# First pair of an attention and gated-MLP kernel on zero-padded operands, extra TensorE products, and a planner with backward passes

## The chip, the cores and the metric

The kernel runs on one core of a Trainium2 chip. The metric is device time in microseconds (us) of one execution. The core's engines run side by side, each with its own queue of instructions, and wait for one another by semaphores: TensorE (PE in the profile; PEld is its weight load), VectorE (DVE), ScalarE (ACT), GpSimd (POOL), and SyncE (SP), whose queue here issues all transfers.

## The reference

Self-attention with queries averaged in pairs, and behind it an MLP with a spatial gate. Batch 8, 8 heads, 1152 keys, 576 pooled queries, head size 64, all f32.

```python
q_pool = q.reshape(B, H, S // 2, 2, D).mean(axis=3)
scores = np.matmul(q_pool, k.transpose(0, 1, 3, 2)) / np.sqrt(D)
attn = np.exp(scores - np.max(scores, axis=-1, keepdims=True))
attn = attn / (np.sum(attn, axis=-1, keepdims=True) + 1e-09)
x = heads_merged(np.matmul(attn, v))          # (8, 576, 512)
h = np.maximum(x @ w_in, 0.0)                 # (8, 576, 1024)
u, g = h[..., :512], h[..., 512:]
g = (g - mean(g)) / np.sqrt(var(g) + 1e-06)   # over the last axis
g = np.einsum('ts,bsd->btd', w_spatial, g) + b_spatial[None, :, None]
out = (u * g) @ w_out                         # (8, 576, 512)
```

## The kernel before

**Pairs.** Attention goes over 32 pairs of heads (i = 0 to 31, four pairs to a batch). f32 operands are split in two f16 numbers, a head and a residual, so that products run at f16 rate. For each pair:

- `prep(i)` loads queries and keys of both heads, stacked on 128 partitions (64 for each head), sums the query pairs on POOL, takes sums of squares on ACT, derives power-of-two scales (`scales`: one tiny product, three DVE steps), and makes heads (`head`, ACT) and residuals (`rest`, DVE, or POOL). Products want head and residual of one attention head stacked on the 128 rows, so transfers copy rows between partitions: `khi` (key heads twice), `qhi` (query head over query residual), `klo` and `xq` (key residual against query head in 64 rows, and two rows more that carry the shift of the softmax).
- `maxima(i)` forms the scores' heads in 27 products of 128 queries by 384 keys (9 query tiles by 3), each reduced by DVE (L751) out of a PSUM bank. Banks `pm` (two) and, in the first unit, `pw` (two) take turns. For pairs 0 and 1 (`DIRECT = 2`) the first head's products (t < 4) read `xq` and the plain key heads `kn` on 64 rows; t = 4 mixes both heads through `qd`; the rest read the copied `qhi` and `khi`.
- `shift` turns the maxima into the two f16 rows of the shift: four DVE steps, a transposing product (L773), a copy (L775), two transfers into `xq` (L778). It runs behind t = 4 and behind the last tile.
- `attention(i)` makes 18 key tiles of exact scores by two products each (L950 on 128 rows, L951 on 66), an exp on ACT (L956) and a subtraction on POOL (L976) that leaves the low half of each f32 in its place. The 64 queries left over of each head are four tail tiles (L963, L967, L972). `values` multiplies high and low halves by head and residual of v, four products each (L853, L859, L864; L846 in f32 for three key tiles of nine in pairs 0 to 7).

**Scheduling of generators.** While `attention(i)` steps, `maxima(i + 1)`, the values' preparation, `prep(i + 2)` and the input weights' conversion (`in_weights`, from pair 0 on at 0.14 steps a tick) step beside it. After two batches a `gated_unit` does the MLP for them, at half a step a tick, in `pw`.

**What sets the order.** The program order of these generators is only the input of a planner, `Order.pin`. It gives each instruction a cost, goes through time, and at each step takes for the engine that is free first the earliest instruction in program order whose inputs are due. "Due" adds an allowance (`SLACK`) to the modelled end where the result crosses to TensorE: 1400 ns from POOL, 300 from ACT, 400 from DVE, 1000 from SP. The order found is fixed for each engine; the hardware's queues then run in it, each waiting at its head. ACT's order up to the end of `prep(0)` and SP's order up to `order.line` are held as written.

**The start.** As written: loads of pair 0, four loads of v, `prep(0)` whole (the next pair's loads among its last steps), 18 steps of `maxima(0)`, the sums of squares of v, the rest of `maxima(0)`, `prep(1)`, the weights' first loads, the first split of v.

## Time and profile before

| | us |
|---|---|
| median of 3 runs | 1167.14 |
| the runs | 1171.51, 1166.41, 1167.14 |
| profiled execution, its time | 1172.69 |
| profiled execution, its span | 1170.9 |
| TensorE busy | 1139.1 (97%) |
| ACT, DVE, POOL busy | 891.6, 858.7, 846.5 |

The page's busy time of TensorE runs from a matmul's start to its end, and matmuls overlap, so rates are read from the distance of two starts. Slices of 1/40 of the span show TensorE at 40% and 90% or more of the first two, and at 90% or more from then on but for the last; the granted clock (PEclk, tenths of full speed) is 7 in the second slice, 9 in the first and full behind it.

### The profile page before, as it was taken

To read this page: it belongs to the slowest core of one execution; us is meant where nothing else is said; L and a number is where in the kernel's file an instruction comes from. 1 tells how busy PE (TensorE), PEld (TensorE's weight loads), DVE (VectorE), ACT (ScalarE), POOL (GpSimd) and SP (SyncE) were. 2 spreads that over 40 slices of the span, in tenths; PEclk is the share of its full clock that TensorE was granted. 3 is DMA by queue.
4 is the path that set the end of the run, shared out by engine and by line. 5 is a ranking of instruction groups with operands and counts; after the bars stand their busy time and mean duration, and the time that the engine had idled before them with its cause. 6 is when DMAs were issued, how large, how long until landed. Compare 5 with 4: busy or idle time off the path is not lost.

```text
span 1170.9 us, 33542 instructions
## 1 busy us (share of the span) xinstructions
PE 1139.1 (97%) x13297; PEld 723.9 (62%) x13297; DVE 858.7 (73%) x2240; ACT 891.6 (76%) x1697; POOL 846.5 (72%) x732
## 2 busy tenths in 40 slices
PE   4999999999999999999999999999999999999998
PEld 1567777776566666666666666666666666665453
DVE  5699999867899878766678668866668777832644
ACT  6698789988787978788777977978777877754423
POOL 3566566778887988889787978898788877883000
PEclk9799999999999999999999999999999999999999
DMA  6575456444432443565323454265433431121002
GB/s 217 153 210 147 111 164 205 139 118 139 125 107 73 122 144 103 140 180 143 90 71 85 139 133 122 69 168 163 115 104 82 127 88 20 38 65 37 1 1 81
DMA packets 88990, 132.97 MB, mean 114 GB/s; under 512 B 39872, under 2 KB 48064, under 8 KB 88832
## 3 DMA queue, kind: packets, MB, share of 16 engines
q1 hardware_dynamic: 88832, 130.82, 39.8%
q8 instruction: 104, 1.70, 0.6%
q14 instruction: 54, 0.44, 0.1%
HBM read 81.20 MB, written 9.44 MB: 77 GB/s over the span
## 4 chain that ended last, share of the span: by engine, by line
PE 82%; DVE 7%; DMA 4%; ACT 3%; POOL 1%; issue 1%; SPq 1%; DVEq 0%; ACTq 0%; POOLq 0%
PE pss L950 9%; PE pss L951 9%; PE pm L745 8%; PE pw L1190 7%; PE pw L1147 7%; PE pw L1103 6%; PE pw L1036 6%; PE o L853 5%; PE o L864 5%; PE o L859 5%; DVE mt L751 3%; PE o L846 2%; PE pss L1036 1%; PE pss L1147 1%; DMA kt<-in_kT_dram 1%; PE pss L1190 1%
## 5 line engine op out<-in xcount | busy, mean ns | idle before, releaser
L976 POOL TENSOR_TENSOR pt<-pt 128x512 f16<-128x512 f32 x528 | 580.9, 1115 | 173.2 <-ACT pt L956 167.8
L956 ACT ACTIVATE pt<-pss,esc 128x512 f32<-128x512 f32 x576 | 389.2, 690 | 115.4 <-PE pss L951 107.9
L751 DVE TENSOR_REDUCE mt<-pm 128x1 f32<-128x384 f32 x733 | 387.5, 549 | 106.3 <-PE pm L745 90.6
L950 PE MATMUL pss<-qhi,khi 128*128 128x512 f16 x576 | 220.6, 383 | 3.9 <-ACT ptl L972 2.1
L951 PE MATMUL pss<-xq,klo 66*128 66x512 f16 x576 | 221.1, 384 | 0.0
L745 PE MATMUL pm<-khi,qhi 128*128 128x384 f16 x643 | 198.1, 326 | 5.2 <-DMA khi<-kn 3.4
L853 PEld LDWEIGHTS <-pt 128*128 128x128 bf16 x2112 | 125.1, 99 | 68.4 <-issue 3.0
L853 PE MATMUL o<-vp,pt 128*128 128x65 f16 x2112 | 157.3, 193 | 1.5 <-DVE xm L872 1.5
L864 PE MATMUL o<-vp,pt 128*128 128x65 f16 x2112 | 154.7, 193 | 0.0
L859 PE MATMUL o<-vp,pt 128*128 128x64 f16 x2112 | 153.1, 193 | 1.1 <-DVE vp L405 1.1
L864 PEld LDWEIGHTS <-pt 128*128 128x128 f16 x2112 | 113.7, 98 | 36.6 <-issue 1.8
L859 PEld LDWEIGHTS <-pt 128*128 128x128 bf16 x2112 | 101.8, 98 | 3.8 <-issue 1.2
L745 PEld LDWEIGHTS <-qhi 128*128 128x128 f16 x744 | 71.1, 99 | 45.6 <-issue 7.1
L1036 PE MATMUL pw<-wi_h,xg 128*128 128x512 f16 x240 | 89.2, 378 | 0.0
L1103 PE MATMUL pw<-xg,wi_h 128*128 128x512 f16 (+1 forms) x336 | 82.6, 325 | 0.0
L751 DVE TENSOR_REDUCE mt<-pw 128x1 f32<-128x384 f32 x131 | 70.4, 546 | 16.5 <-PE pw L745 11.6
L976 POOL TENSOR_TENSOR ptl<-ptl 128x1152 f16<-128x1152 f32 x32 | 69.9, 2184 | 17.4 <-ACT ptl L972 17.4
L972 ACT ACTIVATE ptl<-pss,esc 128x256 f32<-128x256 f32 (+1 forms) x128 | 64.1, 500 | 23.7 <-PE pss L967 23.7
L1147 PE MATMUL pw<-ws_h,vv 128*128 128x512 f16 x216 | 79.2, 379 | 0.0
L1190 PE MATMUL pw<-wo_h,vv 128*128 128x512 f16 x216 | 78.5, 378 | 0.0
L951 PEld LDWEIGHTS <-klo 66*128 66x128 f16 x576 | 56.4, 98 | 31.1 <-issue 8.6
L950 PEld LDWEIGHTS <-khi 128*128 128x128 f16 x576 | 56.5, 98 | 21.3 <-issue 4.3
(255 smaller groups left out, 2503.8 us busy)
## 6 DMA issues: line engine op xcount, KB each, us to landing
vt<-in_v_dram SPq DMA_DIRECT2D x56, 576.0 KB
qt<-in_qT_dram SPq DMA_DIRECT2D x32, 576.0 KB
kt<-in_kT_dram SPq DMA_DIRECT2D x32, 576.0 KB
khi<-kn SPq DMA_DIRECT2D x128, 144.0 KB
out_dram<-row SPq DMA_DIRECT2D x24, 256.0 KB
qhi<-xq SPq DMA_DIRECT2D x64, 72.0 KB
klo<-klo SPq DMA_DIRECT2D x32, 144.0 KB
u<-in_w_in_dram SPq DMA_DIRECT2D x3, 1024.0 KB
```

The lines of the kernel that those rows point to most:

```text
L745: nc.tensor.matmul(pm[:, :W], lhsT=q[:, c0 : c0 + P], rhs=k[:, n * NB : (n + 1) * NB, :], start=True, stop=True,)
L751: nc.vector.reduce_max(out=mt[:, t, n : n + 1], in_=pm[:, :W], axis=AX.X)
L853: nc.tensor.matmul(o[:, t], lhsT=top[:, cols], rhs=vp[:, D : D + D1], start=c == 0 and t == 0, stop=False, skip_group_check=True,)
L859: nc.tensor.matmul(o[:, t, 0:D], lhsT=top[:, cols], rhs=vp[:, 0:D], start=False, stop=False, skip_group_check=True)
L864: nc.tensor.matmul(o[:, t], lhsT=rst[:, cols], rhs=vp[:, D : D + D1], start=False, stop=c == NC - 1, skip_group_check=True,)
L950: nc.tensor.matmul(o, lhsT=khh[:, h, c, :], rhs=qhl[:, h, q], start=True, stop=False)
L951: nc.tensor.matmul(o, lhsT=KL[0:KR, h, c, :], rhs=X[0:KR, h, q], start=False, stop=True)
L956: nc.scalar.activation(pt, ps, AF.Exp, bias=0.0, scale=esc)
L976: nc.gpsimd.tensor_sub(t.bitcast(F16)[..., 0::2], t, t.bitcast(BF16)[..., 1::2])
L1036: nc.tensor.matmul(ph, lhsT=rows(xa, cc, c0, c0 + P), rhs=wa[:, cc, DH:DF], start=n == 0, stop=n == 3 * NCC - 1,)
L1147: nc.tensor.matmul(pv, lhsT=l, rhs=r[:, 0:MAIN], **fl)
L1190: nc.tensor.matmul(py, lhsT=ga[:, fc, c0 : c0 + P], rhs=wa[:, fc, :], start=m == 0, stop=m == end - 1)
```

## The change

1. **First pair.** `prep(0)` writes its query heads into a tile that is zero outside each head's 64 rows (`xz`, in the third `qhi` tile's place). All of its maxima products but those of t = 4 read `xz` and the plain keys `kn` on 128 rows. The first five key blocks are scaled on DVE, not ACT. `klo` and `xq` of this pair are zero in the rows that are not used, and its exact products go over 128 rows. The first shift is made behind t = 3 (`cut = 4`). The first pair's tail tiles start four steps later.
2. **Extra products.** Ahead of the reduction of each of its 27 maxima products the program has a product of 256 columns of `kn` with itself into the bank `o` (`hot`), which nobody reads.
3. **Planner.** The allowances change, costs of some DVE forms are set anew, TensorE's cost follows a model of its clock, and four passes are made: each further pass ranks the ready instructions by a backward pass over the plan before (`backward`) instead of by program order. DVE's order in the first maxima is held as written.
4. **Smaller edits.** The conversion of the input weights begins at pair 4 in the program, at 0.4 steps a tick. The first batch's sums of squares of v take one instruction for a pair of heads, not two. The small scaling of `lnp` goes from DVE to POOL in all pairs.

How the order moves at three places:

TensorE (PE), the end of the first pair's first half of maxima and the start of the second half; `qd` and `qhi` are query tiles, `kn` the plain keys, `khi` the copied ones, `wide` the shift's operand. Before:

```order
L732 MATMUL pw_233<-kn_162,qd0_122 128x384
L773 LDWEIGHTS wide0_133
L773 MATMUL pw_233<-ident_h_94,wide0_133 128x128
L378 LDWEIGHTS ones_96
L378 MATMUL pm_255<-vt_253,ones_96 128x1
L745 LDWEIGHTS qhi0_119
L745 MATMUL pm_264<-khi0_116,qhi0_119 128x384
```

and now:

```order
L868 MATMUL o_143<-kn_167 128x256
L891 LDWEIGHTS wide0_137
L891 MATMUL pm_235<-ident_h_94,wide0_137 128x128
L461 LDWEIGHTS ones_96
L461 MATMUL pm_262<-vt_260,ones_96 128x1
L846 LDWEIGHTS qd0_124
L846 MATMUL pm_282<-kn_167,qd0_124 128x384
L861 LDWEIGHTS qhi2_123
L861 MATMUL pw_294<-kn_167,qhi2_123 128x384
```

The second half's products read `kn` where they read the copies `khi`; one product of t = 4 comes behind the shift's, and products into `o` stand ahead of it.

SyncE (SP), the first pair's transfers around the first shift's two rows (`mr`). Before:

```order
L673 DMA klo_107<-klo_107 64x1152
L674 DMA qhi_119<-xq_113 64x576
L675 DMA xq_113<-xq_113 64x576
L676 DMA khi_116<-kn 64x1152
L677 DMA khi_116<-kn 64x1152
L678 DMA klo_107<-klo_107 2x1152
L778 DMA xq_113<-mr 1x5x128 x2
```

and now:

```order
L761 DMA klo_107<-khi_120 64x1152
L629 DMA kt<-in_kT_dram 128x1152
L896 DMA xq_114<-mr 1x4x128 x2
L767 DMA qhi_121<-qhi_121 64x576
L769 DMA xq_114<-qhi_123 64x576
L770 DMA qhi_121<-qhi_123 64x576
L771 DMA khi_118<-kn 64x1152
L772 DMA khi_118<-kn 64x1152
L773 DMA klo_107<-khi_120 64x1152
```

The rows of the shift stand ahead of the second head's copies, no longer behind them.

VectorE (DVE), behind the first shift of the second pair, while the third pair is prepared (`vv` there is the input weights' tile). Before:

```order
L405 SCALAR_TENSOR_TENSOR qhi2_121<-qt_262,qks_527,xq2_115 128x576
L775 CAST mr_560<-pw_524 10x128
L751 TENSOR_REDUCE mt_367<-pm_634 128x1
L422 TENSOR_SCALAR vv_348<-vv_348 128x1024
L751 TENSOR_REDUCE mt_367<-pw_625 128x1
L751 TENSOR_REDUCE mt_367<-pw_642 128x1
L687 TENSOR_SCALAR lnp_604<-lnp_604 128x1
L405 SCALAR_TENSOR_TENSOR klo2_109<-kt_340,qks_527,kn_611 128x640
L425 SCALAR_TENSOR_TENSOR vv_348<-vv_348 128x1024
```

and now:

```order
L488 SCALAR_TENSOR_TENSOR qhi2_123<-qt_269,qks_546,xq2_116 128x576
L869 TENSOR_REDUCE mt_398<-pw_652 128x1
L869 TENSOR_REDUCE mt_398<-pw_669 128x1
L869 TENSOR_REDUCE mt_398<-pm_679 128x1
L869 TENSOR_REDUCE mt_398<-pm_710 128x1
L869 TENSOR_REDUCE mt_398<-pw_699 128x1
L869 TENSOR_REDUCE mt_398<-pw_713 128x1
L869 TENSOR_REDUCE mt_398<-pm_722 128x1
L488 SCALAR_TENSOR_TENSOR klo2_109<-kt_378,qks_546,kn_640 128x640
```

The weights' rows and the scaling of `lnp` are gone from here; the first of the weights' rows now comes with the second shift of the third pair.

The diff, cut to its core:

```diff
-    SLACK = {("Pool", "PE"): 1400, ("Activation", "PE"): 300, ("DVE", "PE"): 400, ("SP", "PE"): 1000}
+    SLACK = {("Pool", "PE"): 227, ("Activation", "PE"): 90, ("DVE", "PE"): 471, ("SP", "PE"): 1710, ("Activation", "Pool"): 100}
     DELAY = {("PE", "Activation"): 114, ("Activation", "Pool"): 77}
+    WINDOW, COLD, WARM = 3413.3, 0.34, 0.765
+    PASSES = 4
...
-                    n = min(n for n in ns if at[n] <= t)
+                    t = max(f, min(at.values()))
+                    n = min((n for n in ns if at[n] <= t), key=rank.__getitem__)
...
+    def backward(self, g, begin, own):
+
+        lane, cost = g.lane, g.cost
+        size = len(lane)
+        left = [len(after) for after in g.after]
+        ready = {e: [n for n in range(size) if lane[n] == e and not left[n]] for e in self.LANES}
+        due, done = [0.0] * size, [0.0] * size
+        free = dict.fromkeys(self.LANES, 0.0)
+        for _ in range(size):
+            best = None
+            for e, ns in ready.items():
+                if ns:
+                    t = max(free[e], min(due[n] - own[n] for n in ns))
+                    if best is None or t < best[0]:
+                        n = max((n for n in ns if due[n] - own[n] <= t), key=begin.__getitem__)
+                        best = (t, e, n)
+            _, e, n = best
+            ready[e].remove(n)
+            done[n] = free[e] = max(free[e] + own[n], due[n])
+            for pre, through in ((g.before[n], True), (g.begun[n], False)):
+                for m in pre:
+                    x = done[n]
+                    if through and lane[m] != e:
+                        x += cost[m][1] + self.DELAY.get((lane[m], e), 52)
+                    elif through and e != "PE":
+                        x += cost[m][1] + 34
+                    due[m] = max(due[m], x)
+                    left[m] -= 1
+                    if not left[m]:
+                        ready[lane[m]].append(m)
+        return [-t for t in done]
...
+        rank = range(len(prog))
+        for k in range(self.PASSES):
+            if k:
+                rank = self.backward(g, begin, own)
+            turns, begin, own, span = self.forward(g, rank)
...
-    for t in klo:
+    for t in klo[1:]:
         nc.gpsimd.memset(t[D:KR, 1], -MROW)
+    nc.vector.memset(klo[0][D:P], 0.0)
+    nc.vector.memset(klo[0][D:KR], -MROW)
     xq = [const.tile([P, 2, S], F16, name=f"xq{i}") for i in range(NSET)]
+    nc.vector.memset(xq[0][D:P], 0.0)
...
+    for h in range(2):
+        nc.vector.memset(qhi[NSET - 1][(1 - h) * D : (2 - h) * D, h], 0.0)
...
+        if b == 0:
+            src = vt.rearrange("p h c d -> p (h c d)")
+            square_sum(vsq[b][:, hp : hp + 1], src, ws_l[:, 0:2].rearrange("p c s -> p (c s)"))
+            yield
...
+        if i == 0:
+            xz, kl = qhi[NSET - 1], khi[NSET - 1][:, 0]
+            kn = ld.tile([P, NC, P], F16, name="kn")
+            nc.vector.tensor_scalar_mul(kn[:, 0:5], k0[:, 0:5], s_k)
+            head(xz[lower, 0], q0[lower], s_q[lower])
+            head(kn[:, 5:NC], k0[:, 5:NC], s_k)
+            head(xz[upper, 1], q0[upper], s_q[upper])
+            st.update(xz=xz, kn=kn)
+            nc.sync.dma_start(out=qhl[lower, 0], in_=xz[lower, 0])
+            nc.sync.dma_start(out=khh[lower, 0], in_=kn[lower])
+            nc.sync.dma_start(out=khh[upper, 0], in_=kn[lower])
+            for h, (a, rows) in enumerate(((MAIN, lower), (0, upper))):
+                nc.sync.dma_start(out=qd[0][rows, h], in_=xz[rows, h, a : a + TAIL])
+            nc.sync.dma_start(out=X[lower, 0], in_=xz[lower, 0])
+            for a, z in ((0, 5), (5, NC)):
+                nc.scalar.activation(k0[:, a:z], k0[:, a:z], AF.Copy, bias=0.0, scale=s_k)
+                nc.gpsimd.tensor_sub(kl[:, a:z], k0[:, a:z], kn[:, a:z])
+            nc.sync.dma_start(out=KL[lower, 0], in_=kl[lower])
+            factors(st, s, r)
+            load_kq(1)
+            yield
+            rest(qhl[lower, 1], q0[lower], s_q[lower], xz[lower, 0])
+            rest(qhl[upper, 1], q0[upper], s_q[upper], xz[upper, 1])
+            nc.sync.dma_start(out=qhl[upper, 0], in_=qhl[lower, 1])
+            yield
+            nc.sync.dma_start(out=X[lower, 1], in_=xz[upper, 1])
+            nc.sync.dma_start(out=qhl[lower, 1], in_=xz[upper, 1])
+            nc.sync.dma_start(out=khh[lower, 1], in_=kn[upper])
+            nc.sync.dma_start(out=khh[upper, 1], in_=kn[upper])
+            nc.sync.dma_start(out=KL[lower, 1], in_=kl[upper])
+            yield
+            return
...
+        cut = 5 if i else 4
...
-                    if i < DIRECT and h == 0:
+                    if i == 0:
+                        q, k = st["xz"][:, h], st["kn"]
+                    elif i == 1 and h == 0:
                         q, k = X[0:D, 0], st["kn"][0:D]
...
+                if i == 0:
+                    nc.tensor.matmul(hot[:, :256], lhsT=st["kn"][:, 0], rhs=st["kn"][:, 0:2], start=True, stop=True)
...
-            if t == 4:
-                yield from shift(st, mt, pm, 0, 5)
-        yield
-        yield from shift(st, mt, pm, 5, NT)
+            if t == cut - 1:
+                yield from shift(st, mt, pm, 0, cut)
+        yield
+        yield from shift(st, mt, pm, cut, NT)
...
-    W_RATE = 0.14
-    W_AT = 4
+    W_RATE = 0.4
+    W_PAIR = 4
...
+        rows = P if i == 0 else KR
...
-            nc.tensor.matmul(o, lhsT=KL[0:KR, h, c, :], rhs=X[0:KR, h, q], start=False, stop=True)
+            nc.tensor.matmul(o, lhsT=KL[0:rows, h, c, :], rhs=X[0:rows, h, q], start=False, stop=True)
...
-            if k in (1, 2, 3, 4):
-                tail_tile((k - 1) % 2, (k - 1) // 2)
+            j = k if i else k - 4
+            if j in (1, 2, 3, 4):
+                tail_tile((j - 1) % 2, (j - 1) // 2)
...
+    hot = ps_o.tile([P, MAIN], F32, name="o")
     load_kq(0)
     norms = [norm_v(i) for i in range(NHP)]
     for n in norms:
         next(n)
-    drain(prep(0))
-    order.in_turn(tc)
+    load_kq(1, True)
+    ready = prep(0)
+    for _ in range(5):
+        next(ready)
+    order.in_turn(tc, "Activation")
     first = maxima(0)
-    for _ in range(18):
+    for _ in range(13):
         next(first)
+    order.in_turn(tc, "DVE")
+    for _ in range(2):
+        next(first)
+    drain(ready)
     for n in norms:
         drain(n)
     load_kq(2, True)
+    drain(split_v(0))
     drain(first)
     drain(prep(1))
     weights = in_weights()
     next(weights)
-    drain(split_v(0))
     order.line(tc)
...
-            Pace(weights, W_RATE, W_AT if i == 0 else 0),
+            Pace(weights if i >= W_PAIR else None, W_RATE),
```

208 lines of the change are left out of this document (119 added, 89 removed).

## The prediction

> **What bounds the kernel now.** I read the page first, then the stages, then the first 60 us engine by engine.
>
> ```profile
> span 1170.9 us, 33542 instructions
> ...
> PE 1139.1 (97%) x13297; PEld 723.9 (62%) x13297; DVE 858.7 (73%) x2240; ACT 891.6 (76%) x1697; POOL 846.5 (72%) x732
> ...
> ```
>
> ```profile
> 0.00:60.00 60.00, 42.48 (x300) 21.86 (x301) 37.40 (x96) 41.53 (x80) 29.19 (x36) 0.86 0.60 181
> 60.00:200.00 140.00, 132.55 (x1648) 98.53 (x1647) 132.96 (x335) 121.38 (x232) 89.91 (x71) 1.00 0.57 165
> 200.00:400.00 200.00, 197.54 (x2425) 130.84 (x2424) 169.84 (x433) 172.94 (x340) 164.57 (x137) 1.00 0.44 126
> 400.00:1060.00 660.00, 659.32 (x8229) 419.18 (x8226) 467.65 (x1259) 514.27 (x970) 555.78 (x484) 1.00 0.40 107
> 1060.00:1171.00 111.00, 107.18 (x712) 53.51 (x708) 50.82 (x120) 41.50 (x78) 7.06 (x7) 1.00 0.09 29
> ```
>
> In the stages the numbers behind the length are the busy us of PE, weight loads, DVE, ACT and POOL, then the granted clock. TensorE is idle for 17.5 us of the first 60, 7.5 of the next 140, 2.5 of the next 200, 0.7 of the next 660, and 3.8 at the end, where nothing is changed. So only the start can give much: an instruction saved on DVE after 200 us is hidden behind TensorE. The start holds a second loss that idle time does not show, in the clock:
>
> ```profile
> 20.10:23.70 3.60, 0.23 (x2) 0.07 (x2) 0.58 (x4) 2.69 (x6) 0.00 (x0) 1.00 0.61 128
> 26.90:33.60 6.70, 5.27 (x57) 3.15 (x57) 6.63 (x18) 5.97 (x10) 3.79 (x4) 1.00 0.12 46
> 33.70:50.70 17.00, 17.00 (x80) 7.50 (x80) 9.03 (x18) 8.10 (x16) 9.85 (x9) 0.50 0.74 195
> 50.80:56.40 5.60, 5.60 (x71) 4.10 (x70) 3.02 (x14) 5.29 (x12) 3.87 (x4) 1.00 0.45 176
> ```
>
> ```profile
> 8.52 0.16 PE L378 MATMUL pm<-sq,ones 128*128 128x2 bf16 x1 [8.52 <-ACT klo L399]
> 10.72 0.48 PE L745 MATMUL pw<-kn,xq 64*128 64x384 f16 x1 [2.04 <-ACT kn L402]
> ...
> 23.75 0.48 PE L745 MATMUL pm<-khi,qhi 128*128 128x384 f16 x1 [3.42 <-DMA khi<-kn]
> 24.03 0.52 PE L745 MATMUL pw<-khi,qhi 128*128 128x384 f16 x1
> 24.35 0.52 PE L745 MATMUL pm<-khi,qhi 128*128 128x384 f16 x1
> ...
> 30.86 0.23 PE L773 MATMUL pw<-ident_h,wide 128*128 128x128 f16 x1 [0.18 <-DVE wide L769]
> 32.18 0.28 PE L859 MATMUL o<-vp,pt 128*128 128x64 f16 x4 [1.09 <-DVE vp L405]
> ...
> 44.92 0.63 PE L950 MATMUL pss<-qhi,khi 128*128 128x512 f16 x1
> 45.35 0.63 PE L951 MATMUL pss<-xq,klo 66*128 66x512 f16 x1
> ...
> 54.11 0.38 PE L951 MATMUL pss<-xq,klo 66*128 66x512 f16 x1
> 54.33 0.38 PE L950 MATMUL pss<-qhi,khi 128*128 128x512 f16 x1
> ...
> 56.39 0.22 PE L773 MATMUL pw<-ident_h,wide 128*128 128x128 f16 x1
> ```
>
> From 33.7 to 50.7 us the clock is 0.50 and TensorE is never idle: 512 columns step by 0.43 us (44.92 to 45.35), against 0.22 later (54.11 to 54.33). At 24 us 384 columns step by 0.32 us, which is also the half rate, though the clock column reads 1.00 there; it records no change before 26.8 us, so I go by steps. The 17 us would be 8.5 at full clock. I measure everything at one milestone, the transposing matmul of the second pair's first maxima, at 56.39 us (the pair before has its second at 30.86).
>
> The chain of waits says what sets the time before that:
>
> ```profile
> 18.02 5.60 DMA khi<-kn
> ...
> 23.75 0.49 PE pm L745
> ...
> 24.27 5.67 DVE mt L751 x12
> ...
> ```
>
> The first head's maxima need no copied rows, the second head's do. The last copy is issued at 18.02 and ends the wait at 23.75; then twelve reductions, 0.47 us each, set the pace.
>
> **The change part by part.**
>
> *First pair without row copies.* All 27 maxima products read one zero-padded query tile and the plain keys, so none waits for a copy. Ahead of that DVE fills 1152 + 576 + 2304 + 2 x 288 = 4608 elements more per partition.
>
> ```profile
> L515 DVE MEMSET ws_l<- x1: 298/298/298, 299.2 to 299.2; 64x288 uint32 x1
> ...
> 1.91 1.16 DVE L336 CAST ident_h<-ident 128x128 f16<-128x128 f32 x1 [0.91 <-POOL ident masks.py:199]
> 2.06 2.10 DVE L342 COPY ident<-ident 64x64 f32<-64x64 f32 x2
> 8.72 0.17 DVE L383 TENSOR_SCALAR pm<-pm 128x2 int32<-128x2 int32 x1 [4.57 <-PE pm L378]
> ...
> 9.18 0.77 ACT L402 ACTIVATE xq<-qt,qks 128x576 f16<-128x576 f32 x1 [0.71 <-DVE qks L389]
> 9.86 1.43 ACT L402 ACTIVATE kn<-kt,qks 128x640 f16<-128x640 f32 x2
> ```
>
> At 298/288 = 1.03 ns each that is 4.8 us, from about 1.0 us on; with the identity copies that follow (1.91 to 4.16, 2.2 us) DVE is done near 8.1, and it idles until 8.72, so the fills cost nothing. If they ran 0.6 us longer, every later step would slip by the excess. Then the query head (0.77 us on ScalarE) and the first keys (now on DVE, beside it) are ready together near 10.0, where both heads and keys stood in one ScalarE queue before: the first product moves from 10.72 to about 10.0. Twelve reductions end near 10.5 + 12 x 0.47 = 16.1, the shift (four small DVE steps, the transpose, a copy: 1.5 us, and half a residual of 0.8) lets the fifteen others start near 18.4; with three small steps for the value scale and two residuals before the last of them they end at 18.4 + 15 x 0.47 + 0.4 + 1.6 = 27.5, and the shift behind them puts the milestone's predecessor at 28.3 instead of 30.86: **-2.5 us**. On SP the row writes of the first shift now stand right behind the first pair's transfers of head 0, where before they waited behind the copies of head 1:
>
> ```profile
> 22.86 1.51 SPq L778 DMA_DIRECT2D xq<-mr  x2
> ```
>
> Now they can go at about 18, as soon as the rows exist, and what queues behind them (the copies for head 1) is needed only by tiles after 30 us. If the key load of the second pair ahead of them were late, nothing would change, since issuing does not wait for landing.
>
> *The 256-column products.* 27 of them, 256/1.2 = 0.213 us each at half and 0.107 at full rate (from the 0.32 and 0.16 that 384 columns take). They stand between maxima products whose pace is the reduction's 0.47 us, on an engine that would idle, so 2.9 to 5.8 us of TensorE work cost nothing there. The cover is thin while the clock is low: the order puts 14 of them ahead of the twelfth product, 12 x 0.32 + 14 x 0.213 = 6.8 us against 5.6 of reductions, so up to 1.2 us if the clock does not rise within them. They keep TensorE full from 10.0 on; in the trace the clock rose after a stretch like that (23.75 to 26.9), so I expect full rate by 13 to 17 us, and then the dense work from 25 us on at full rate.
>
> *The cold stretch.* At full rate its 17.0 us of matmuls shrink to 8.5, but the row above it says that POOL was busy for 9.85 of them, DVE for 9.03, ACT for 8.10. The same work cannot take less than 9.9, so I take **-7.1 us**; bounds 0 (the others' waits fill the hole) and -8.5. The wait of 1.09 us for the value residual (32.18) I leave in.
>
> Whether the clock stays up is decided between 18 and 25 us, where the order has 13 products and hardly any of the new ones: 0.16 us of work per 0.47, or 34%.
>
> ```profile
> 30.20:33.60 3.40, 2.12 (x19) 1.00 0.04 10
> ```
>
> Behind this window, busy for 2.12 of 3.40 us, the clock fell. Summed by their steps, its matmuls stream for about 1.5 us, 43% of it, more than half of that in four-pass f32. So 34% is at the edge: price 0 to 3.4 us (two stretches of 3.4 us at half rate), taken as 0 in the sum. The Trainium skill, TensorE: Matmul & The Clock Gate, Part 1 (The HAM clock gate), has the clock fall only after at least one idle window of about 3.4 us; this trace contradicts that, since the window before the fall was mostly busy. By the page nothing is lost here, by the row up to 3.4 us.
>
> *Weights later, a new order.* The conversion of the input weights, four pieces of six DVE instructions of about 1.2 us, stood from the second pair on; now it starts a pair later and is spread to pair 7, and 32 small scalings go to POOL.
>
> ```profile
> L432 DVE SCALAR_TENSOR_TENSOR u<-u 128x1024 int32<-128x1024 int32 x3 | 3.6, 1210 | 0.0
> ...
> PE pss L950 <- ACT ptl L972: 2.1, 3, 1.2
> PE pss L950 <- ACT pt L956: 1.7, 5, 0.7
> PE pm L378 <- ACT klo L399: 1.5, 1, 1.5
> ```
>
> These waits are TensorE's longest from 60 to 200 us, where DVE is busy for 133 of 140. Counting DVE instructions of the order between shifts with this trace's durations, pairs 2 to 5 carry 20 to 23 us instead of 22 to 26, beside 21 to 26 of TensorE. Bounds 0 and all of the 7.5 idle us; TensorE becomes the longer one, but the waits named are for ACT, which gains only in part: about half, **-3.5 us**.
>
> *Thinner margins.* The planner's allowance from POOL to TensorE falls from 1400 to 227 ns, from ACT from 300 to 90.
>
> ```profile
> L976 POOL TENSOR_TENSOR pt<-pt 128x512 f16<-128x512 f32 x528 | 580.9, 1115 | 173.2 <-ACT pt L956 167.8
> L956 ACT ACTIVATE pt<-pss,esc 128x512 f32<-128x512 f32 x576 | 389.2, 690 | 115.4 <-PE pss L951 107.9
> ```
>
> Exp and subtraction take 0.69 + 1.12 us, an estimated 2.0 with hand-offs. Summing matmul steps along the order, the median TensorE work between a tile's second product and the first use of its low half is 5.2 us before and 5.1 after, for one tile in twenty it is under 3.8 and 3.3. Most tiles keep cover; a few will wait behind a busy POOL. Bounds 0 and 0.05 us for each of 528 tiles, 26 us; near the first, since only 0.7 us are idle from 400 to 1060: **+2 us**.
>
> Sum: -2.5 - 7.1 - 3.5 + 2 = -11.1 us. Against the profiled execution's own 1172.69 us (1.8 outside its span) that is 1161.6. That execution is 5.6 above the median of the runs. The three runs spread by 5.1 us, as much as three cold stretches of 3.4 us would cost at 1.7 each; if its excess is such cold time, the change removes it here and the median's gain is smaller, 1161.6; if not, the median goes to 1156.0. Between them I forecast **1158 us**, 0.8% faster.
>
> **The rivals.** *The clock falls again* in the maxima's second half or comes late: for it, 34% at an unknown edge; against it, dense work follows at once. 1158 + 3.4 = 1161. *The gain is taken back at once*: with TensorE at full rate, DVE and ACT become the bound before 60 us; for it, DVE's 133 of 140 behind the milestone; against it, 9 of 17 in the cold stretch. Then -2.5 and some 2 us stay: 1163. *Slower*: TensorE waits at the first low-half product of each tile, because the order brings it closer than POOL delivers; for it, POOL is busy for 556 of 660 us; against it, the distances above. It outweighs the 11.1 + 5.8 us from 32 ns per tile on; at 0.05 us it is 1158 - 2 + 26 = 1182, with half the tiles 1169.
>
> **How the numbers follow.** Forecast 0.64, its own range 1150 to 1163; clock falls 0.12; taken back 0.14; waits per tile 0.10. A measurement of this kernel tells about 0.5%, or 5.8 us, from no change: faster is below 1161.3. Faster: 0.57 + 0.06 + 0.03 = 0.66; same: 0.07 + 0.06 + 0.11 + 0.02 = 0.26; slower 0.08. The range for 8 in 10 starts from the lower reading, 1156, less the idle time that the 3.5 us leave (4.0), the rest of the cold stretch (1.4) and the margins' 2: 1148. It ends at the higher reading, 1161.6, with the clock's 3.4 us and 3 us of the waits per tile: 1168.
>
> **What would show it.** Right: the first product near 10.0, no wait for khi in the first pair, 256-column products at 0.107 us from 13 to 17 us on, clock 1.00 from there to the end, the milestone near 46.8 us, under 5 us idle between 60 and 200, about 99% busy later. Wrong: a 0.50 stretch after 20 us, a milestone past 50, or TensorE waiting for POOL's low halves after 400 us by more than 5 us in all.

## The result, and the profile after

The changed kernel takes 1181.9 us (median of 4 runs, 1174.75 to 1182.97) against 1169.3 for the kernel before (4 runs): ratio 1.010, 95% interval 1.0054 to 1.0147. The forecast was 1158 us, so the sign was wrong too. One number of the kernel before needs a sentence: of its 100 executions that were timed with the experiments, 73 have a mean granted clock of 0.997 or more (median 1167.4 us) and 26 one of 0.994 or less (median 1171.0 us), and the profiled one (1172.69 us, 0.992) is like the second group.

The page of the changed kernel, its span and the engines' busy time:

```profile
span 1181.2 us, 33615 instructions
...
PE 1140.7 (97%) x13324; PEld 728.0 (62%) x13324; DVE 873.7 (74%) x2207; ACT 895.1 (76%) x1697; POOL 872.6 (74%) x771
```

Its stages, in the columns of the prediction (length; busy us of PE, weight loads, DVE, ACT, POOL with their counts; clock; transfers):

```profile
0.00:60.00 60.00, 46.12 (x447) 28.73 (x448) 49.71 (x122) 45.20 (x82) 34.50 (x42) 0.94 0.69 206
60.00:200.00 140.00, 131.04 (x1644) 98.60 (x1641) 129.63 (x309) 124.13 (x239) 107.25 (x85) 1.00 0.55 156
200.00:400.00 200.00, 195.02 (x2383) 128.87 (x2380) 172.12 (x423) 171.28 (x336) 165.63 (x142) 0.99 0.47 127
400.00:1060.00 660.00, 651.09 (x8021) 411.51 (x8019) 470.06 (x1229) 507.54 (x958) 550.74 (x491) 0.99 0.39 106
```

TensorE's idle time went from 17.5 to 13.9 us in the first 60, and then up: 7.5 to 9.0, 2.5 to 5.0, and 0.7 to 8.9 between 400 and 1060. The counts say where the time went. Added up, and less the 27 extra products, the changed kernel has started 420 products at 60 us, 2064 at 200, 4447 at 400, 12468 at 1060; the kernel before 300, 1948, 4373, 12602. The lead is 120, 116, 74 and then -134 products; at the 12.5 per us of the late stage (8229 in 660 us) that is 9.6 us of lead at the start and 10.7 us of lag at 1060, which is the difference of the spans (10.3). The start delivered; what followed gave back twice as much.

One edit of the change is missing in its description: from pair 4 on, no longer from pair 8 on, ACT and POOL make the keys' residuals that DVE made (`if i < 4` stands for `if i < EARLY`). POOL's 107.25 us in the second stage (89.91 before) come from it in the main: the kernels below that keep this edit have 96 to 109 us there, those without it 89 to 92.

The start on TensorE:

```profile
10.03 0.50 PE L861 MATMUL pw<-kn,qhi 128*128 128x384 f16 x1 [1.33 <-ACT qhi L485]
10.32 0.64 PE L868 MATMUL o<-kn 128*128 128x256 f16 x2
...
14.97 1.25 PE L868 MATMUL o<-kn 128*128 128x256 f16 x10
...
29.73 0.23 PE L891 MATMUL pw<-ident_h,wide 128*128 128x128 f16 x1 [0.51 <-DVE wide L887]
...
47.88 0.22 PE L891 MATMUL pw<-ident_h,wide 128*128 128x128 f16 x1
```

The first product stands at 10.03 (10.72 before), the milestone at 47.88 (56.39), and no product of the first pair waits for a copied row. The clock by stretches, in the columns of the stages:

```profile
13.00:16.40 3.40, 3.22 (x26) 2.36 (x24) 3.40 (x8) 3.34 (x7) 3.02 (x4) 1.00 0.62 125
16.40:19.80 3.40, 1.99 (x10) 0.93 (x11) 3.11 (x14) 1.83 (x5) 0.39 (x1) 1.00 0.63 199
19.80:26.60 6.80, 6.80 (x18) 2.02 (x17) 6.77 (x14) 6.77 (x14) 0.26 (x1) 0.50 0.44 98
...
525.00:531.80 6.80, 4.67 (x53) 2.62 (x52) 2.79 (x9) 3.31 (x7) 2.47 (x4) 1.00 0.59 160
531.90:535.20 3.30, 3.30 (x30) 2.14 (x29) 1.93 (x6) 2.30 (x5) 1.83 (x3) 0.50 0.97 379
```

It rises at 13 us (384 columns step by 0.32 us until then and by 0.16 from then on), falls again at 19.8 for 6.8 us, and, which the profiled execution of the kernel before does not show, falls three times later (231, 532 and 702 us) for 3.4 us each, each time behind a hole in TensorE's work.

What makes the holes. ScalarE's waits for the key loads in the changed kernel, in us in all, times and longest:

```profile
ACT klo L482 <- DMA kt<-in_kT_dram: 28.7, 16, 4.7
```

The same view of the kernel before:

```profile
ACT klo L399 <- DMA kt<-in_kT_dram: 14.0, 12, 4.3
```

The first pair's own 4.3 us are in this one; in the changed kernel the first pair's wait has a line of its own (4.4 us), so it is 9.7 against 28.7. L482 (L399) is the sum of squares of a pair's keys, the first thing that is done with a load (`kt`). Two of these loads in the changed kernel's chain of waits (start, length, what):

```profile
222.32 6.66 DMA kt<-in_kT_dram
...
522.52 5.95 DMA kt<-in_kT_dram
```

The second on ACT's timeline:

```profile
523.09 0.69 ACT L1076 ACTIVATE pt<-pss,esc 128x512 f32<-128x512 f32 x1 [0.17 <-PE pss L1071]
528.49 1.16 ACT L482 ACTIVATE klo<-kt 128x1152 f16<-128x1152 f32 x1 [4.71 <-DMA kt<-in_kT_dram]
```

And on PE's:

```profile
528.57 0.38 PE L1311 MATMUL pw<-wo_h,vv 128*128 128x512 f16 x1
530.38 0.30 PE L971 MATMUL o<-vp,pt 128*128 128x65 f16 x4 [1.43 <-ACT pt L1076]
```

From 523.8 to 528.5 ACT does nothing: the sum of squares stands at the head of its queue before its load has landed, the exponentials (L1076) stand behind it, TensorE waits for their tiles (`pt`), and the clock falls at 532. TensorE's longest waits between 400 and 1060 us in the changed kernel:

```profile
PE o L971 <- ACT pt L1076: 2.8, 2, 1.4
PE o L982 <- POOL pt L1096: 2.7, 4, 0.7
PE pss L1083 <- ACT pt L1076: 1.9, 2, 1.7
```

### The profile page after: what moved, and what is told of

It reads as the page before. It is cut to its first block, busy times and chain, and to the rows that moved or that the text cites. A ratio compares the mean times of both kernels' runs of the same rounds, so it can differ in the third digit from the quotient of the medians.

```text
span 1181.2 us, 33615 instructions
## 1 busy us (share of the span) xinstructions
PE 1140.7 (97%) x13324; PEld 728.0 (62%) x13324; DVE 873.7 (74%) x2207; ACT 895.1 (76%) x1697; POOL 872.6 (74%) x771
## 4 chain that ended last, share of the span: by engine, by line
PE 72%; DVE 8%; DMA 5%; ACT 5%; POOL 3%; issue 2%; SPq 1%; ACTq 0%; DVEq 0%; POOLq 0%
PE pss L1070 8%; PE pss L1071 8%; PE pm L861 7%; PE pw L1224 6%; PE pw L1268 6%; PE pw L1157 6%; PE pw L1311 5%; DMA kt<-in_kT_dram 4%; PE o L982 4%; PE o L971 4%; PE o L977 4%; DVE mt L869 3%; ACT pt L1076 2%; POOL pt L1096 2%; PE o L964 1%
## 5 line engine op out<-in xcount | busy, mean ns | idle before, releaser
L1076 ACT ACTIVATE pt<-pss,esc 128x512 f32<-128x512 f32 x576 | 390.3, 692 | 114.4 <-PE pss L1071 99.8
L1071 PE MATMUL pss<-xq,klo 66*128 66x512 f16 (+1 forms) x576 | 220.1, 383 | 0.0
L861 PE MATMUL pm<-khi,qhi 128*128 128x384 f16 x637 | 195.1, 326 | 2.0 <-DVE xg L938 1.3
L982 PEld LDWEIGHTS <-pt 128*128 128x128 f16 x2112 | 110.3, 98 | 27.4 <-POOL pt L1096 6.4
L861 PEld LDWEIGHTS <-qhi 128*128 128x128 f16 x756 | 74.0, 101 | 61.2 <-issue 10.8
L1071 PEld LDWEIGHTS <-klo 66*128 66x128 f16 (+1 forms) x576 | 56.5, 98 | 31.3 <-issue 10.7
L818 POOL TENSOR_TENSOR klo<-kt,kn 128x640 f16<-128x640 f32 (+1 forms) x56 | 74.6, 1334 | 1.1 <-ACT kn L817 1.1
```

What stands on the lines that cost most here:

```text
L861: nc.tensor.matmul(pm[:, :W], lhsT=q[:, c0 : c0 + P], rhs=k[:, n * NB : (n + 1) * NB, :], start=True, stop=True,)
L982: nc.tensor.matmul(o[:, t], lhsT=rst[:, cols], rhs=vp[:, D : D + D1], start=False, stop=c == NC - 1, skip_group_check=True,)
L1071: nc.tensor.matmul(o, lhsT=KL[0:rows, h, c, :], rhs=X[0:rows, h, q], start=False, stop=True)
L1076: nc.scalar.activation(pt, ps, AF.Exp, bias=0.0, scale=esc)
```

## The experiments

Four theories, by the numbers that the expectations use. **Theory 1**: the planner puts ACT's sum of squares right at the modelled landing of the key load, with no allowance from SP to ACT; the load comes later, and ACT's queue, then PE, stands. **Theory 2** (the prediction's slower rival, widened): the thin margins from POOL and ACT to PE cost. **Theory 3**: it is the order, not the edits; the order of the kernel before is a tight one, and whatever changes the program or the planner's numbers exchanges it for another. **Theory 4**: the edits themselves cost time later.

### The planner's margins and passes, and the first pair without the new planner

```diff
-    SLACK = {("Pool", "PE"): 227, ("Activation", "PE"): 90, ("DVE", "PE"): 471, ("SP", "PE"): 1710, ("Activation", "Pool"): 100}
+    SLACK = {("Pool", "PE"): 227, ("Activation", "PE"): 90, ("DVE", "PE"): 471, ("SP", "PE"): 1710, ("Activation", "Pool"): 100, ("SP", "Activation"): 3000}
```

> The changed kernel with one more margin in the table of slacks: an instruction of ACT is placed no sooner than 3000 ns after the modelled landing of a load that it reads. Theory 1 (ACT's queue is lined up with the modelled landing of the key load, the load comes later, the exponentials behind the sum of squares stand still and PE with them): ACT's idle time before the sum of squares of keys that is put down to the load falls from 28.7 us to under 12 us, PE's idle time between 400 and 1060 us from 8.9 us to under 4, and the time from about 1182 us to 1165 to 1172 us. Theory 2 (the margins from POOL and ACT to PE are too thin): these margins stay thin, so PE's idle time there stays at 7 to 10 us and the time at 1178 to 1184 us.

Measured 1170.4 us, ratio to the kernel before 1.0016 (0.9999 to 1.0033). ACT waits for no key load but the first pair's; PE is idle for 4.7 us between 400 and 1060.

```diff
-    SLACK = {("Pool", "PE"): 227, ("Activation", "PE"): 90, ("DVE", "PE"): 471, ("SP", "PE"): 1710, ("Activation", "Pool"): 100}
+    SLACK = {("Pool", "PE"): 1400, ("Activation", "PE"): 300, ("DVE", "PE"): 400, ("SP", "PE"): 1000}
```

> The changed kernel with the old table of slacks (POOL to PE 1400, ACT to PE 300, DVE to PE 400, SP to PE 1000, none from ACT to POOL), backward passes kept. Theory 2 (thin margins): PE's waits for POOL's and ACT's tiles are gone, PE's idle time between 400 and 1060 us falls from 8.9 to about 2 us, and the time to 1163 to 1168 us. Theory 1 (late key loads on ACT's queue): the sum of squares of keys still waits about 25 us in all for its loads, and the time stays at 1176 to 1184 us.

Measured 1191.7 us, 1.0200 (1.0162 to 1.0239): the thick margins make it worse, with 22.2 us of ACT's waits for keys and 11.4 us of idle PE. Theory 2 falls in this form.

```diff
-    PASSES = 4
+    PASSES = 1
```

> The changed kernel with one forward pass in program order, so without the backward passes that rank the instructions; margins and costs stay the new ones. Theory 1 in its full form (the ranking by latest start is what moves the sum of squares of keys up to the landing of its load): ACT's idle time put down to the key load falls from 28.7 us to 8 to 15 us, and the time to 1164 to 1171 us. Theory 2 (thin margins): margins are as thin as before, so the time stays above 1175 us.

Measured 1177.2 us, 1.0071 (1.0044 to 1.0099); ACT waits 22.0 us for keys, PE is idle for 4.0. The expectation missed: the ranking is not what puts the squares at the landing.

```diff
-    SLACK = {("Pool", "PE"): 227, ("Activation", "PE"): 90, ("DVE", "PE"): 471, ("SP", "PE"): 1710, ("Activation", "Pool"): 100}
-    WINDOW, COLD, WARM = 3413.3, 0.34, 0.765
-    PASSES = 4
+    SLACK = {("Pool", "PE"): 1400, ("Activation", "PE"): 300, ("DVE", "PE"): 400, ("SP", "PE"): 1000}
...
-    W_RATE = 0.4
-    W_PAIR = 4
+    W_RATE = 0.14
+    W_AT = 4
```

> The planner, its costs and margins and the pacing of the weights' work as in the kernel before; of the change only the first pair's new operands, the 256-column products, the order of the start and the factor that POOL computes now. If the loss comes from the planner alone (theories 1 and 2): the second pair's first shift product begins 7 to 9 us sooner than the kernel before has it (at 47 to 50 us), PE's idle time between 400 and 1060 us is back at 0.7 to 2 us, the key loads cost ACT about 11 us, and the time is 1158 to 1163 us, below the kernel before. If the new first pair itself upsets what follows: the time is 1168 us or more.

Measured 1174.7 us, 1.0045 (1.0027 to 1.0063), with ACT's waits at 10.6 us and PE's idle time at 4.9. The milestone is at 52.28 us, not at 47 to 50: the clock falls twice in the start, for 6.8 us at 19.5 and for 10.2 us at 36.6. This was the surprise: with the old planner, and with ACT's waits near those of the kernel before, these edits still end 0.45% behind. They are more than the expectation names, since the kernel also keeps the key residuals of pairs 4 to 7 on ACT and POOL and the joined sums of squares of v. Either the edits cost (theory 4) or the old planner's order is lost with any edit (theory 3).

### The order against the edits

To hold an order, a kernel carries a table of the instructions of each engine as another kernel issues them, and each kept instruction may begin only behind the one before it:

```diff
+        for e, steps in table.items():
+            mine = [n for n in range(len(prog)) if names[prog[n].engine] == e]
+            k, prior = 0, None
+            for d in steps:
+                k += d
+                if prior is not None and prior not in before[mine[-k]]:
+                    begun[mine[-k]].add(prior)
+                prior = mine[-k]
```

In the first such kernel the old part, from about 190 us on, is instead set whole behind the new one, which is planned alone.

> The new first pair (with the 256-column products, the new planner with the 3000 ns margin on ACT's loads, the factor back on DVE, the old pacing of the weights' work) up to about 190 us; every instruction that the kernel before issues after about 190 us stands on its engine in exactly the order of the kernel before. Theory 3 (the order that the old planner had found for the last 900 us is an unusually tight one, and any change of the program loses it, whichever planner orders it): PE's idle time between 400 and 1060 us goes from 4 to 9 us (in the changed kernel and its variants so far) to 0.5 to 2 us, and the time is 1160 to 1165 us, below the kernel before. Theory 4 (the first pair's edits themselves cost time later): PE's idle time there stays at 4 us or more and the time at 1168 us or more.

Measured 1171.1 us, 1.0018 (1.0002 to 1.0034). The idle time is as theory 3 has it, the time is not: PE is idle for 9.2 us between 60 and 200, with a stretch of 6.8 us at half clock from 64.7. That may be the seam, or the key residuals of pairs 4 to 7, which this kernel still has on ACT and POOL; the two were not separated. Its stage from 400 us on:

```profile
400.00:1060.00 660.00, 659.51 (x8219) 419.00 (x8216) 465.46 (x1255) 512.03 (x967) 555.34 (x484) 1.00 0.39 107
```

0.5 us idle, with the new first pair ahead of it. The other way round, nothing of the change and one number of the old planner:

```diff
-    SLACK = {("Pool", "PE"): 1400, ("Activation", "PE"): 300, ("DVE", "PE"): 400, ("SP", "PE"): 1000}
+    SLACK = {("Pool", "PE"): 1400, ("Activation", "PE"): 300, ("DVE", "PE"): 420, ("SP", "PE"): 1000}
```

> The kernel before with nothing of the change; one margin of its planner, from DVE to PE, is 420 instead of 400 ns, which sets most of its instructions in another order. Theory 3 (tight order by luck of the plan): PE's idle time between 400 and 1060 us rises from 0.7 us to 3 to 9 us and the time from about 1169 to 1172 to 1180 us. Theory 4: the time stays within 0.3% of the kernel before (1166 to 1172 us), since no edit of the change is in it.

Measured 1182.6 us, 1.0117 (1.0086 to 1.0148): 20 ns on one margin cost as much as the whole change did. The same stage of this kernel, 5.5 us idle:

```profile
400.00:1060.00 660.00, 654.47 (x8126) 413.32 (x8125) 471.58 (x1267) 513.05 (x968) 547.38 (x477) 1.00 0.39 106
```

And one edit of the change alone, first with a new order and then with the old one held:

```diff
-            nc.vector.tensor_scalar(
+            nc.gpsimd.tensor_scalar(
                 out=lnp, in0=lnp, scalar1=math.log(PEXP) / ESC, scalar2=2.0 ** 29, op0=ALU.mult, op1=ALU.min
             )
```

> The kernel before with one edit of the change alone: the factor of each pair (a product and a minimum on 128x1 elements) is computed by POOL instead of DVE, old planner and old margins. Theory 3: as with any other change of the program, the order changes and the time rises to 1172 to 1180 us, with PE's idle time between 400 and 1060 us at 3 to 9 us. Theory 4 with this edit as the cost: the same rise, but then the kernel with one altered margin does not rise. A rise in neither points to the first pair's operands.

> The kernel before with the factor of each pair on POOL instead of DVE, as in the kernel with that edit alone (1179.3 us), but every other instruction on every engine in exactly the order of the kernel before. Theory 3 (the order costs, not the edit): back at 1166 to 1171 us, PE's idle time between 400 and 1060 us at 0.5 to 2 us. Theory 4 (the edit costs): 1176 us or more.

Measured 1179.3 us, 1.0096 (1.0063 to 1.0129), planned anew; 1168.4 us, 1.0009 (0.9999 to 1.0020), with every other instruction in its old place. The edit costs nothing; the order that it brings costs 11 us. The stages of the second:

```profile
0.00:60.00 60.00, 40.24 (x355) 23.25 (x356) 45.48 (x106) 44.52 (x87) 31.11 (x40) 1.00 0.65 191
60.00:200.00 140.00, 134.88 (x1673) 99.91 (x1672) 133.39 (x326) 123.60 (x238) 91.81 (x78) 0.99 0.58 172
200.00:400.00 200.00, 197.66 (x2432) 131.12 (x2431) 168.61 (x431) 174.18 (x343) 169.38 (x145) 1.00 0.43 119
400.00:1060.00 660.00, 659.71 (x8211) 418.53 (x8210) 461.63 (x1228) 510.92 (x961) 559.76 (x501) 1.00 0.39 107
```

This execution is also what the profiled one of the kernel before was not, the same order without the long stretch at half clock (one of 3.4 us, at 60.2, is left). The changed planner moves as easily:

```diff
-    SLACK = {("Pool", "PE"): 227, ("Activation", "PE"): 90, ("DVE", "PE"): 471, ("SP", "PE"): 1710, ("Activation", "Pool"): 100}
+    SLACK = {("Pool", "PE"): 227, ("Activation", "PE"): 90, ("DVE", "PE"): 480, ("SP", "PE"): 1710, ("Activation", "Pool"): 100}
```

> The changed kernel with one of its new margins, from DVE to PE, at 480 instead of 471 ns. Theory 3 (each plan of the whole program is a draw whose time scatters by several us, and the changed kernel's is one draw): the time moves by more than 3 us in either direction from 1182, most likely to between 1170 and 1180 us. If the new margins and the backward passes themselves fix the loss: 1179 to 1185 us, as the changed kernel.

Measured 1189.0 us, 1.0170 (1.0126 to 1.0213), 7 us above the changed kernel by 9 ns of margin, and in the other direction than I thought likely. The two ratios' intervals touch (1.0147 and 1.0126), but all four runs (1185.1 to 1190.7) lie above all four of the changed kernel.

### The key loads within the changed kernel's own order

Here the whole order of the changed kernel is held. First a second buffer for the keys. To make room for it, this kernel and the two behind it leave out the gate's bias (a row of the gate's weights stands in its place) and 16 small copies on DVE. They so compute another output with a little less work; what they show is read from one to the next.

```diff
-        kt = ld.tile([P, KEYS], F32, name="kt")
+        kt = ld.tile([P, KEYS], F32, name="kt", bufs=2)
```

> The changed kernel with every instruction on every engine in exactly its order, and a second buffer for the keys' load, so that a load no longer waits until POOL and DVE have read the pair before (to make room for it, the gate's bias is replaced by a row of the gate's weights and 16 small copies of DVE are left out). Theory 1 (late key loads stop ACT's queue, and with it PE): ACT's idle time before the sum of squares of keys falls from 28.7 us to under 10 us, PE's idle time between 400 and 1060 us from 8.9 us to under 4 us, and the time from about 1182 to 1168 to 1174 us. If the loads are late for another reason or ACT's wait is not what PE feels: PE's idle time stays above 7 us and the time at 1178 us or more.

Measured 1177.2 us, 1.0080 (1.0056 to 1.0103), and ACT's waits for the key loads are still there:

```profile
ACT klo L587 <- DMA kt<-in_kT_dram: 27.4, 14, 4.8
```

So the occupied buffer is not why the loads are late; their place in SP's queue is the next suspect. With the second buffer, and each load from the fourth on ten places earlier in SP's order:

> The changed kernel with every instruction of PE, ACT, DVE and POOL in exactly its order, with the second buffer for the keys' load (and what was left out for it: the gate's bias and 16 small copies of DVE), and each key load from the fourth on ten places earlier in SP's queue. Theory 1 (ACT's wait for the key loads stops PE): ACT's idle time before the sum of squares of keys falls from 27.4 us (with the second buffer alone) to under 8 us, PE's idle time between 400 and 1060 us from 8.7 us to under 4 us, and the time from 1177 to 1164 to 1171 us. If ACT's wait goes and PE's idle time stays above 7 us and the time above 1175 us, PE waits for something else and theory 1 falls.

Measured 1174.4 us, 1.0053 (1.0031 to 1.0076). ACT's waits fall to 0.2 us and PE's idle time between 400 and 1060 from 8.7 to 2.4 us, but the early loads, moved ahead of the row copies, bring a wait of 4.3 us for `qhi<-qhi` and two stretches of 6.8 us at half clock (58 and 92 us). The same with the loads from the ninth on alone:

> As the kernel with the key loads ten places earlier in SP's queue (order of PE, ACT, DVE and POOL that of the changed kernel, second buffer for the keys, gate's bias and 16 copies left out), but only the loads from the ninth on, which are issued after about 185 us: the start and the first 185 us keep SP's order too. Theory 1 (the late key loads cost about 6 us after 300 us): ACT's idle time before the sums of squares after 200 us is gone, no stretch at half clock near 58 and 92 us, and the time is 1168 to 1172 us against 1177 with the second buffer alone. If the gain of the earlier loads is taken back elsewhere: 1174 us or more.

Measured 1170.3 us, 1.0007 (0.9990 to 1.0024). The same wait of ACT, and the stage from 400 us on:

```profile
ACT klo L587 <- DMA kt<-in_kT_dram: 3.0, 2, 2.3
```

```profile
400.00:1060.00 660.00, 656.15 (x8166) 416.41 (x8164) 465.96 (x1222) 510.04 (x958) 554.88 (x497) 1.00 0.38 107
```

The only difference to the kernel with the second buffer is the place of 24 loads in SP's queue: ACT's waits go from 27.4 to 3.0 us, PE's idle time from 8.7 to 3.9, the one late fall of the clock (3.4 us at 529) is gone, and 7 us with them; the intervals of the two ratios lie apart. Theory 1 holds for that much of the loss.

### What is left of the start's gain, and of the other margin

The old order from 190 us on, with overlap allowed at the seam:

> As the kernel with the old order from about 190 us on, except that the new first part is no longer finished before the old part begins: the planner may let the two overlap, with the old part's own order kept on each engine. If the loss of that kernel between 60 and 200 us against the kernel before (a stretch at half clock from 64.7 us and one wait of 3.6 us for a copy of the queries) came from the seam: it goes, and the time is 1162 to 1167 us, below the kernel before. If not: 1168 to 1173 us, with PE's idle time between 400 and 1060 us below 2 us all the same.

Measured 1175.8 us, 1.0071 (1.0054 to 1.0088), PE idle for 0.1 us between 400 and 1060. The late stage is the old one; with the overlap the stage before it is worse (129.6 us busy of 140 between 60 and 200, 130.8 without). The 256-column products alone, in the old order:

```diff
+                if i == 0:
+                    nc.tensor.matmul(hot[:, :256], lhsT=st["kn"][:, 0], rhs=st["kn"][:, 0:2], start=True, stop=True)
                 nc.vector.reduce_max(out=mt[:, t, n : n + 1], in_=pm[:, :W], axis=AX.X)
```

> The kernel before with every instruction in exactly its order and the 27 products of 256 columns alone, one behind each product of the first pair's maxima. If they bring the clock up earlier and keep it (full rate from 13 to 17 us, no stretch at half rate from 33.7 us): 2 to 5 us below the kernel before, 1163 to 1166 us. If they only fill PE's waits: no difference, within 1.5 us of the kernel before.

Measured 1175.6 us, 1.0064 (1.0039 to 1.0088), 5 runs from 1171.4 to 1178.4. Its first stage:

```profile
0.00:60.00 60.00, 44.05 (x378) 25.23 (x378) 44.16 (x107) 43.14 (x86) 30.46 (x36) 1.00 0.63 188
```

Of 378 products 27 are the extra ones: 351 of the kernel's own by 60 us, against 355 without them (the kernel with the factor on POOL, above). They make this kernel slower, by more than their 2.9 us of column time. In the execution shown the clock is at 1.00 from 23 us on and does not fall, but they don't secure that: two of the five runs, with a mean clock of 1.000, take 1171.4 and 1172.3 us, three, at 0.991 or less, 1175.6 to 1178.4. Without them, in the change with the load margin:

> The changed kernel with the 3000 ns margin on ACT's loads and without the 256-column products (and without the tile that they write). If these products bring PE's clock up earlier, as in the changed kernel (full rate from 13.02 us): here the granted clock is 0.50 until 20 us or later, the first pair's products step at twice the time, and the time is 3 to 8 us above that of the same kernel with them (1170.4). If they only cost: about 2.9 us less column time and 1167 to 1169 us.

Measured 1179.8 us, 1.0090 (1.0064 to 1.0115), but by a new order again, so the time says nothing of the products. The clock does, in this kernel's stretches:

```profile
10.40:13.80 3.40, 3.29 (x10) 1.14 (x9) 3.16 (x7) 3.35 (x7) 1.45 (x2) 1.00 1.05 349
13.90:17.20 3.30, 0.82 (x3) 0.10 (x1) 3.09 (x10) 3.21 (x7) 2.18 (x3) 1.00 0.50 118
17.30:24.10 6.80, 6.23 (x17) 1.95 (x18) 6.64 (x19) 4.71 (x10) 0.26 (x1) 0.50 0.42 123
```

The trace has the rise at 13.9 us without them and the fall at 17.3. The same kernel with them (the first run above) rises at 15.5 and holds the rate until 199.8; the changed kernel rises at 13.0 and falls at 19.8. With the order held from 60 us on, with them and without:

> The new first pair with the 256-column products, planned alone; every instruction that the kernel before issues after about 60 us stands on its engine in its old order (so the residuals of keys of the pairs 4 to 7 are back on DVE, the factor is on DVE and the weights' work has its old pacing). Theory 3: PE's idle time between 400 and 1060 us is 0.5 to 2 us. If the start's gain survives the seam: 1161 to 1166 us, below the kernel before; if the old order waits for its own engines where the new start is early: 1167 to 1172 us.

> The kernel with the old order from about 60 us on, without the 256-column products. If these products gain by the clock in the new start: 2 to 5 us slower than the same kernel with them. If they only add column time to a PE that is busy 99% later (27 products of 0.107 us, 2.9 us): 1 to 3 us faster.

Measured 1171.9 us, 1.0033 (1.0012 to 1.0054), with them; 1170.3 us, 1.0020 (1.0004 to 1.0035), without. By 60 us 366 and 367 products of the kernel's own have started. The medians are 1.6 us apart and the intervals overlap: what the extra products cost or bring in the new start isn't settled. What they do to the clock shows in this pair, whose order from 60 us on is the same. With them:

```profile
17.06 0.33 PE L949 MATMUL pw<-kn,qhi 128*128 128x384 f16 x1
```

Without them:

```profile
17.19 0.48 PE L949 MATMUL pm<-kn,qhi 128*128 128x384 f16 x1
```

The clock rises at 15.65 us with them and at 26.32 without; with them it falls again, from 22.48 to 25.89, and the milestones are at 52.22 and 51.87 us. Both are later than the changed kernel's 47.88, so the new operands alone do not give that start. PE is idle for 0.1 and 1.0 us between 400 and 1060. Last, the margin from POOL, on top of the margin for ACT's loads:

```diff
-    SLACK = {("Pool", "PE"): 227, ("Activation", "PE"): 90, ("DVE", "PE"): 471, ("SP", "PE"): 1710, ("Activation", "Pool"): 100, ("SP", "Activation"): 3000}
+    SLACK = {("Pool", "PE"): 1400, ("Activation", "PE"): 90, ("DVE", "PE"): 471, ("SP", "PE"): 1710, ("Activation", "Pool"): 100, ("SP", "Activation"): 3000}
```

> The changed kernel with the 3000 ns margin on ACT's loads (1170.4 us) and the margin from POOL to PE back at 1400 ns from 227. If thin margins from POOL cost what is left (theory 2: PE's largest wait there after 60 us is for POOL's tiles, 4.9 us): that wait falls below 1.5 us and the time is 1163 to 1167 us, below the kernel before. If a margin is worth less than the draw of a new order (theory 3): 1172 to 1182 us, with the wait for POOL gone and others in its place.

Measured 1173.1 us, 1.0038 (1.0022 to 1.0053), 2.7 us above the same without it (the intervals overlap). Not even PE's wait that it should cover went; it was 4.9 us without the margin:

```profile
PE o L982 <- POOL pt L1096: 6.0, 5, 2.8
```

No run beat the kernel before.

### All of them by who made the late order

| | PE idle, 400 to 1060 us | time, us |
|---|---|---|
| old order held (kernel before; five kernels with edits ahead of or in it) | 0.7; 0.5, 0.1, 0.4, 0.3, 0.1 | 1167 to 1169; 1171, 1176, 1176, 1168, 1172 |
| the same, without the 256-column products | 1.0 | 1170 |
| planned anew, old planner (first pair alone; margin 420; factor on POOL) | 4.9, 5.5, 3.0 | 1175, 1183, 1179 |
| planned anew, new planner (the change; load margin; old margins; one pass; no 256; margin 480; POOL's margin) | 8.9, 4.7, 11.4, 4.0, 5.6, 11.5, 9.1 | 1182, 1170, 1192, 1177, 1180, 1189, 1173 |

All ten new plans are idle for 3.0 us or more in this stage, all seven kernels with the old order for 1.0 or less, whatever the edits. That is theory 3. Two edits were never set into the old order, the later conversion of the input weights and the key residuals of pairs 4 to 7, but neither has an instruction in this stage: in the changed kernel the residuals are done by 190 us, and the first product that reads the converted weights starts at 252.9. So theory 4 falls for the late stage. The time does not follow this column alone (9.1 us idle go with 1173 us, 0.1 with 1176): the stages before 400 us count as well.

## Why the prediction was wrong, point by point

**Where it failed most: "Thinner margins", +2 us, "near the first" bound.** This was the only term for the later stages of a program that was planned anew as a whole. It priced one margin (POOL to PE) and took PE's 0.7 us of idle time between 400 and 1060 as a sign that little could go wrong; these 0.7 us were a property of the one order that the change threw away. In its place: idle PE from 200 to 1060 us went from 3.1 to 13.9 us, and three stretches of 3.4 us at half clock came on top, some 1.7 us each (not in every execution: one of the changed kernel's four, at a mean clock of 1.000, took 1174.75 us, still above the kernel before). In products, the lead fell by 254 between 60 and 1060 us, some 20 us, where the sum had a gain of 1.5 (-3.5 + 2). About 7 us of this are ACT's waits for the key loads, shown by moving 24 loads in SP's queue. The rest is other waits of the new order (POOL's and ACT's tiles above), of which no single one was tested. The slower rival named the right engine to suffer, and its time (1182) is the measured one by luck, since its mechanism isn't there: PE's waits for POOL's low halves after 400 us are 2.7 us in all, under the 5 that I had set as its sign.

**"The cold stretch", -7.1 us: priced on an execution that is not the usual one.** In the same order without that stretch (the factor on POOL) the milestone is at

```profile
49.71 0.22 PE L858 MATMUL pw<-ident_h,wide 128*128 128x128 f16 x1
```

so 6.7 of the 8.5 us that the change gains at the milestone are there without it. In products, the lead of 120 at 60 us over the profiled execution is one of 65 over this one (420 against 355): 5 us, not 9.6. I had written down both readings of the 5.6 us by which the profiled execution lay above the median (1161.6 and 1156.0) and put the forecast between them. The runs speak for the first: the excess is in the main cold time, which most executions of the kernel before, by their mean clock, do not have.

**"First pair without row copies", -2.5 us: -1.1.** The first product at 10.03 (forecast 10.0), no wait for copied keys, the shift behind the first pair at 29.73 instead of 28.3. The milestone came out at 47.88 against 46.8.

**"The 256-column products", nothing.** They step by 0.107 us from 13 us on and the clock was at full rate by then, as forecast. In the new start with the old order behind it they bring the rise forward by 10.7 us, but no time that the runs can tell, and in the old start they make the kernel 0.64% slower. Costing them at nothing was too kind for the old start; for the new one it stays open.

**The clock between 18 and 25 us: 0 of 0 to 3.4.** It fell, from 19.8 to 26.6 us, behind a stretch with TensorE busy for 1.99 of 3.40 us. That was one of the prediction's own signs of being wrong. It cost little there, since DVE, with the reductions, was busy for 6.77 of these 6.80 us.

**"Weights later", -3.5 us: +1.5.** DVE is relieved (129.6 us busy of 140 instead of 133.0), but PE is idle for 9.0 us there, not under 5: its longest waits from 60 to 200 us are still for ACT (2.3, 2.2 and 2.1 us), as the bound had warned, and the first of them is for a sum of squares of keys.

## What to carry to other kernels

In a program that a planner orders as a whole, an edit is two changes, the edit and a new order of everything, and the second can be the larger: hold the old order in a table to price the edit, and try the planner with a margin off by a few ns to see how far its orders scatter. An engine that is 99.9% busy in one order promises nothing for the next one. Where a load feeds an in-order queue that others depend on, the planner needs a margin there too, and the load an early place in its own queue. And before a term is put on a stretch of the profiled execution, compare its time and clock with the median of the runs: what only that execution lost can't be gained.

## What the runs showed of the hardware

The clock falls behind stretches in which TensorE worked for a good part of the time: in the changed kernel 1.99 of 3.40 us (16.4 to 19.8) and 1.28 of the 3.41 us before the fall at 531.84. The Trainium skill, TensorE: Matmul & The Clock Gate, Part 1 (The HAM clock gate), asks for a whole idle window; these rows contradict it. Nor does a like stretch always end in a fall: in the same trace TensorE is busy for 1.97 of the 3.41 us from 67.63 on, and the rate stays. The change with the load margin has, behind its rise at 15.5 us,

```profile
18.90:22.30 3.40, 2.49 (x9) 0.84 (x9) 3.40 (x11) 2.09 (x5) 0.00 (x0) 1.00 0.12 32
22.30:25.70 3.40, 2.39 (x10) 0.87 (x9) 3.40 (x9) 3.28 (x8) 0.00 (x0) 1.00 0.61 132
```

and keeps its rate. What decides is not shown. In each trace the changes of the clock lie a whole number of steps of 3.41 us apart (13.0, 19.8, 26.7, ... in the changed kernel), and where the steps begin differs from trace to trace. That whether a hole makes a fall depends on how it lies to these steps would fit that one kernel has executions with and without a long stretch at half clock; it was not tested.

A load of 128 x 1152 f32 (590 KB) took 5.95 and 6.66 us from its issue in the two places of the changed kernel's chain shown above, with other transfers beside it.
